# Batches on consecutive partitions, four plain stores and two loads of x

## The chip, the cores and the metric

The kernel runs on one core of a Trainium2 chip. The metric is the device time of one execution in microseconds (us), as the median of three runs. TensorE is written PE, VectorE DVE, ScalarE ACT, GpSimd POOL and SyncE SP.

## The reference

One decoding step for a batch of 8. A normalised x goes through attention over a window of 1024 cached positions (32 query heads, 8 key heads, 128 wide) and an output projection; beside it x goes through a gated feed-forward block; the two results are multiplied and added to x.

```python
B, Sq, D = 8, 1, 512;  Hq, Hkv, Sk, Dh = 32, 8, 4096, 128;  F = 1792     # all bf16
W = min(4096, max(256, Sk // 4))                                          # 1024
xn = layernorm(x)
q = (xn @ wq)                                # per head
p = softmax(q @ k[:, :, Sk - W:].T * Dh ** -0.5)
s = (p @ v[:, :, Sk - W:]) @ wo
g = silu((gelu(x @ w_gate) * (x @ w_up)) @ w_down)    # B's x is the normalised x
return x + s * g                             # (8, 1, 512)
```

## The kernel before

**Loads.** Some 47 MB are loaded, nearly all of it by SP. The order of issue is the program's: the first quarter of wo (`wo_first`, L106), wq as one load of 4 MB (L109), then for each batch two loads of 1 MB of k and two of v (`load_cache`, L84), then w_gate, w_up (L426) and w_down (L429), and the rest of wo in five loads (L439), the last three of them 640, 256 and 128 KB. ACT issues x alone, in five loads of two or one rows (L79). The destinations of the big loads are a ring of eight slots, and the loads share eight semaphores in turn, which are called lanes here: a load that takes a lane waits for the landing of the load eight places before it, whichever queue issued that.

**The head.** DVE takes the mean and variance of x with one batch on each of 8 partitions (L145 to L152). PE turns the normalised rows into columns (L166), and four copies lay them into `xnR` (L168): for each of four chunks 32 columns, of which the batches take every fourth (`RB = 4`), the rest being zero. So every result with batches on partitions has batch b on partition 32 t + 4 b, where t is the chunk of columns. `xpad` is a mask that lays x itself out in the same way for the last addition (`x_res`). The query product (L260) takes `xnR` as its stationary operand; casts, DVE transposes and 16 copies on DVE and ACT (L283) sort q into `qbd`.

**The batches.** For each batch DVE transposes k in blocks of 32 (`turn_k`, L248), PE makes the scores (L309), DVE and ACT the softmax, DVE transposes the probabilities (L344), and PE applies v (L354). Twice, after four batches each, `regroup` writes the head outputs to `oT` (L395), again with a batch on every fourth of 32 columns.

**The tail.** The gate and up products (L453), GELU, the down product (L482) and the SiLU are made while the rest of wo comes in. The output projection (`s_ps`, L501) runs over 32 blocks of wo rows, four column chunks each, in the order in which wo lands. Two DVE operations follow (`y`, L509, and `out_sb`, L511), and one store takes every fourth partition of `out_sb` (L513):

```python
    nc.sync.dma_start(
        out=out_f.rearrange("b (t d) -> t b d", t=4), in_=out_sb[0 : P : RB, :]
    )
```

L541 is the closing block, in which SP waits for all semaphores in turn and the engines meet.

Of the kernel before, what the change touches and what calls it, by code (L numbers as in the profile page):

```python
# [13 lines left out]
PSUM = bass.MemoryType.PSUM  # L14

N_SLOTS = 8
RB = 4
NEG = -1.0e30


# [1 line left out]
def kernel(  # L22
# [13 lines left out]
    nc = tc.nc  # L36

    B, Sq, D = A_x.shape
# [7 lines left out]
    P = nc.NUM_PARTITIONS  # L46
    NK = D // P
    HG = 4
    NG = Hkv // HG
# [4 lines left out]
    DT = D // 4  # L54
# [20 lines left out]


    x_sb = keep.tile([B, D], BF16, name="x_sb")
    for r, z in ((0, 2), (2, 4), (4, 6), (6, 7), (7, 8)):
        nc.scalar.dma_start(out=x_sb[r:z], in_=A_x.flatten_outer_dims()[r:z])  # L79

    def load_cache(cache, b, name):
# [15 lines left out]
    def load_v(b):  # L97
# [21 lines left out]
        out=ident,  # L119
        in_=ident,  # L120
# [4 lines left out]
        channel_multiplier=1,  # L125
# [3 lines left out]
    xnR = keep.tile([P, NK, 4, 32], BF16, name="xnR")  # L129
# [4 lines left out]
        out=xpad,  # L134
        in_=xpad,
# [1 line left out]
        fill=1.0,  # L137
        base=0,
        pattern=[[-1, 32]],
        channel_multiplier=RB,  # L140
    )


# [9 lines left out]
        out=xhat,  # L153
# [8 lines left out]
    with tc.tile_pool(name="ps_x", bufs=1, space=PSUM) as ps_x:  # L162
        xnT_ps = ps_x.tile([P, NK, B], BF16, name="xnT_ps")
        xv = xhat.rearrange("b (p k) -> b k p", k=NK)
        for k in range(NK):
            nc.tensor.transpose(xnT_ps[:, k, :], xv[:, k, :], ident[0:B, 0:B])  # L166
        for j in range(4):
            nc.vector.tensor_copy(out=xnR[:, :, j, 0 : RB * B : RB], in_=xnT_ps)  # L168
        xr_ps = ps_x.tile([P, DT], FP32, name="xr_ps")
        for t in range(4):  # L170
            nc.tensor.matmul(
                xr_ps[32 * t : 32 * t + 32, :],
                xpad,
                x_sb[:, t * DT : (t + 1) * DT],
                start=True,
                stop=True,
            )
        nc.scalar.copy(out=x_res, in_=xr_ps)  # L178
# [3 lines left out]
    qd = Hq // NG  # L182
# [6 lines left out]
        out=hv,  # L189
        in_=hv,  # L190
# [4 lines left out]
        channel_multiplier=1,  # L195
    )
    nc.gpsimd.affine_select(
        out=neg_st,
        in_=neg_st,
# [4 lines left out]
        channel_multiplier=-1,  # L204
# [3 lines left out]
        out=neg_mv,  # L208
        in_=neg_mv,
# [4 lines left out]
        channel_multiplier=1,  # L214
# [6 lines left out]
    for g in range(NG):  # L221
        nc.vector.tensor_reduce(
            out=sel[:, g, g * qd : (g + 1) * qd],
            in_=ident.rearrange("p (t g h) -> p g h t", t=4, g=NG)[:, g],
# [5 lines left out]
        out=own, in_=ident.rearrange("p (i e) -> p e i", e=8), axis=AX.X, op=ALU.add  # L230
    )
    pick = consts.tile([P, 4 * NU], BF16, name="pick")
    with nc.allow_low_precision(reason="sums of zeros and a single one"):
        nc.vector.tensor_reduce(
            out=pick, in_=ident.rearrange("p (a e) -> p a e", e=8), axis=AX.X, op=ALU.add
        )
    oT = keep.tile([P, 8, NU, 32], BF16, name="oT")
# [5 lines left out]
    qbd = keep.tile([P, 2, B, 2, NG, 4 * Hq], BF16, name="qbd")  # L243
    kT = {}

    def turn_k(b, g):
        t = kT_pool.tile([P, ROW], BF16, name="kT")
        nc.vector.transpose(out=t.bitcast(I32), in_=k_sb[b][:, g].bitcast(I32))  # L248
        kT[b, g] = t
# [5 lines left out]
    q_t = q_both[:, ROW : 2 * ROW]  # L255
    with tc.tile_pool(name="ps_q", bufs=1, space=PSUM) as ps_q:
# [10 lines left out]
        for half in range(2):  # L267
            for i in range(4 * half, 4 * half + 4):
                e = nc.vector.tensor_copy if i % 4 == 3 else nc.scalar.copy
                e(out=q_bf[:, i * 512 : (i + 1) * 512], in_=q_ps[i])  # L270
            for i in range(4 * half, 4 * half + 4, 2):
                sl = slice(i * 512, (i + 2) * 512)
                nc.vector.transpose(out=q_t[:, sl].bitcast(I32), in_=q_bf[:, sl].bitcast(I32))

    wq_ctx.close()
    q_v = q_t.rearrange("p (g h m b r w) -> p m b r w g h", g=NG, h=qd, m=2, b=B, r=RB)
    for j in range(4):
        sl = slice(32 * j, 32 * j + 32)
        for m in range(2):
            for g in range(NG):  # L280
                e = nc.scalar.copy if (4 * j + 2 * m + g) % 3 == 2 else nc.vector.tensor_copy
                c0 = j * Hq + g * qd
                e(out=qbd[sl, m, :, :, g, c0 : c0 + qd], in_=q_v[sl, m, :, 0, :, g, :])  # L283
    turn_k(0, 1)


# [89 lines left out]
    def regroup(q):  # L376

        rc = two.tile([P, 1], FP32, name="rc")
        nc.vector.reciprocal(out=rc, in_=o_ps[q][:, Dh : Dh + 1])
        o_x = two.tile([P, 8, Dh], BF16, name="o_x")  # L380
        nc.vector.scalar_tensor_tensor(
            out=o_x,
            in0=o_ps[q][:, 0:Dh].unsqueeze(1).broadcast_to([P, 8, Dh]),
            scalar=rc,
            in1=own.unsqueeze(2).broadcast_to([P, 8, Dh]),
            op0=ALU.mult,
            op1=ALU.mult,
        )
        ox_v = o_x.rearrange("p h (e j) -> p j (h e)", j=8)
        r_ps = ps_g.tile([P, 8, 4, NU], FP32, name="r_ps")  # L390
        for j in range(8):
            nc.tensor.matmul(  # L392
                r_ps[:, j], ox_v[:, j], pick, start=True, stop=True
            )
        nc.vector.tensor_copy(  # L395
            out=oT[:, :, :, 4 * RB * q : 4 * RB * (q + 1) : RB],
            in_=r_ps.rearrange("p j b u -> p j u b"),
        )

# [2 lines left out]
    for b in range(B):  # L402
        if b + 2 < B:
            load_k(b + 2)
        if b + 1 < B:
            load_v(b + 1)
            turn_k(b + 1, 0)
        softmax(b)
        if b + 1 < B:
            scores(b + 1, 0)  # L410
        if b >= 1:
            gather(b - 1)
        if b + 1 < B:
            turn_k(b + 1, 1)
            scores(b + 1, 1)
        turn_p(b)
        values(b)
        keep_o(b)
        if b == 4:
            regroup(0)  # L420
# [10 lines left out]
    for u in range(1, NU):  # L431
        if u % 2 == 1:
            pair = slot("wo_sb").rearrange("p (v j d) -> p v j d", v=2, d=D)
        t = pair[:, (u - 1) % 2]
# [6 lines left out]

    gather(B - 1)
    regroup(1)
    actx.close()

# [3 lines left out]
    for n, ws in (("z_ps", wgu[0]), ("u_ps", wgu[1])):  # L449
# [15 lines left out]
        out=z2, in0=z2, scalar1=0.044715, scalar2=1.0, op0=ALU.mult, op1=ALU.add  # L465
# [11 lines left out]
        out=hT.rearrange("p j b -> p (j b)"), in_=h_bf.rearrange("p (y j) -> p j y", j=NJ)  # L477
    )
    f_ps = ps_f.tile([P, DT], FP32, name="f_ps")
    for j in range(NJ):  # L480
# [11 lines left out]
        out=g_sb, in0=g_sb, scalar1=0.5, scalar2=0.5, op0=ALU.mult, op1=ALU.add  # L492
# [5 lines left out]
    for u in range(NU):  # L498
# [11 lines left out]
    out_sb = ffn.tile([P, DT], BF16, name="out_sb")  # L510
    nc.vector.tensor_tensor(out=out_sb, in0=y, in1=x_res, op=ALU.add)  # L511
    out_f = out.flatten_outer_dims()
    nc.sync.dma_start(  # L513
        out=out_f.rearrange("b (t d) -> t b d", t=4), in_=out_sb[0 : P : RB, :]
    )


# [28 lines left out]
```

## Time and profile before

| what | value |
|---|---|
| median of 3 runs | 120.96 us (120.95 to 120.99) |
| the profiled execution | 120.95 us, its span 119.1 us |
| busy PE, DVE, ACT, POOL | 69.2, 75.7, 32.9, 3.2 us |
| loaded, and rate over the span | 47.46 MB, 399 GB/s |
| share of the span on the chain that ended last | DMA 77%, PE 11%, DVE 6% |
| mean granted TensorE clock | 0.882 |

Busy times overlap, and the share that matters is that on the chain: the profile follows the last event back to what released it. In the slices each digit stands for a fortieth of the span, 2.98 us, in tenths; the row DMA is the mean share of the 16 DMA engines that were moving data. A line of the timeline gives start, duration, engine, line, operation, destination and source. "ACTq" and "SPq" are issues on ACT's and SP's queue; an issue is the instruction that hands over a transfer, a landing its completion.

### The profile page before, as it was taken

Reading aid. Unit: us, or ns where it says so; the run is one execution under the profiler, and the core shown is the slowest. Engines: PE = TensorE matmul, PEld = TensorE weight load, DVE = VectorE, ACT = ScalarE, POOL = GpSimd, SP = SyncE. Lnnn points to the kernel's source line nnn. Section 1 sums busy time; section 2 is a strip of 40 time slices with the busy share of each in tenths; the row PEclk is TensorE's granted clock in tenths of the full one; section 3 lists DMA queues with packets and bytes.
Section 4 is the critical chain, followed back from the end, with each engine's and each line's share of the span. In section 5 each row is a group of like instructions: output and inputs, shape, how many; then the busy total and the mean of one; then the engine's idle time right before and its main releaser. Section 6 shows DMA issues by size and latency. Waiting matters only on the chain.

```text
span 119.1 us, 1740 instructions
## 1 busy us (share of the span) xinstructions
PE 69.2 (58%) x704; PEld 33.7 (28%) x704; DVE 75.7 (64%) x101; ACT 32.9 (28%) x83; POOL 3.2 (3%) x10
## 2 busy tenths in 40 slices
PE   0000079921699497996967866657358264746550
PEld 0000033400234153442533324233124142206530
DVE  1000487999994999999987995981996114373100
ACT  1300230196100816154261441161081810110000
POOL 2000052000000000000000000000000000000000
PEclk9999999999558999999999999999999855555775
DMA  2998899999999999999999999999999999999930
GB/s 56 474 496 386 369 429 432 424 424 432 426 418 432 429 421 421 432 426 424 427 421 424 429 432 429 421 426 426 421 429 435 444 429 424 433 418 413 421 118 3
DMA packets 6108, 47.57 MB, mean 399 GB/s; under 512 B 717, under 2 KB 853, under 8 KB 1109
## 3 DMA queue, kind: packets, MB, share of 16 engines
q1 hardware_dynamic: 6084, 47.46, 94.6%
q8 instruction: 5, 0.08, 0.2%
q14 instruction: 3, 0.02, 0.0%
q10 hardware_dynamic: 16, 0.01, 0.0%
HBM read 47.46 MB, written 0.01 MB: 399 GB/s over the span
## 4 chain that ended last, share of the span: by engine, by line
DMA 77%; PE 11%; DVE 6%; ACT 2%; ACTq 1%; issue 1%; DVEq 0%; SPq 0%
DMA k_sb<-in_A_k_cache_dram 32%; DMA wo_sb<-in_A_wo_dram 19%; DMA v_sb<-in_A_v_cache_dram 16%; DMA x_sb<-in_A_x_dram 9%; PE q_ps L260 7%; DVE kT L248 4%; PE S_ps L309 2%; ACTq L79 1%; ACT L161 1%; DVE mx L319 1%; PE O_ps L354 1%; DVE stats L145 1%; PE s_ps L501 1%; PE r_ps L392 1%; DVE y L509 0%
## 5 line engine op out<-in xcount | busy, mean ns | idle before, releaser
L309 PE MATMUL S_ps<-kT,qbd 128*128 128x512 bf16 x128 | 33.0, 403 | 17.8 <-DVE kT L248 14.3
L248 DVE STREAM_TRANSPOSE kT<-k_sb 128x2048 int32<-128x2048 int32 x16 | 36.5, 2289 | 4.1 <-DMA k_sb<-in_A_k_cache_dram 4.1
L309 PEld LDWEIGHTS <-qbd 128*128 128x128 bf16 x128 | 12.8, 101 | 35.9 <-issue 19.9
L329 ACT ACTIVATE nb<-m 32x1 f32<-32x1 f32 x32 | 6.4, 201 | 23.7 <-DVE m L326 23.4
L319 DVE TENSOR_REDUCE mx<-S_ps 128x1 f32<-128x1024 f32 x8 | 9.6, 1195 | 2.5 <-PE S_ps L309 2.5
L332 ACT ACTIVATE P_sb<-S_ps,nb 128x1024 bf16<-128x1024 f32 x8 | 11.1, 1388 | 0.3
L354 PE MATMUL O_ps<-v_sb,pT 128*32 128x256 bf16 x256 | 9.3, 292 | 2.7 <-DVE pT L344 2.7
L166 PE MATMUL xnT_ps<-ident,xhat 8*128 8x8 bf16 x4 | 0.3, 174 | 15.0 <-DVE xhat L152 15.0
L260 PE MATMUL q_ps<-wq_sb,xnR 128*128 128x512 bf16 x32 | 8.7, 438 | 0.5 <-ACT x_res L178 0.5
L366 ACT COPY O_sb<-O_ps 128x256 f32<-128x256 f32 x8 | 3.0, 374 | 21.1 <-PE O_ps L354 21.1
L354 PEld LDWEIGHTS <-pT 128*32 128x32 bf16 x256 | 6.5, 102 | 6.3 <-issue 3.0
L145 DVE BATCH_NORM_STATS2 stats<-x_sb 8x6 f32<-8x512 bf16 x1 | 0.7, 681 | 11.8 <-DMA x_sb<-in_A_x_dram 11.8
L344 DVE STREAM_TRANSPOSE pT<-P_sb 128x512 int32<-128x512 int32 x8 | 5.7, 711 | 3.4 <-ACT P_sb L332 2.8
L374 PE MATMUL o_ps<-O_sb,sel 128*32 128x129 f32 x32 | 5.5, 297 | 1.0 <-ACT O_sb L366 1.0
L298 PE MATMUL S_ps<-neg_mv,neg_st 128*128 128x512 bf16 x16 | 4.8, 382 | 2.1 <-DVE q_both L270 2.1
L270 ACT CAST q_both<-q_ps 128x512 bf16<-128x512 f32 x6 | 3.0, 611 | 7.3 <-PE q_ps L260 7.3
L260 PEld LDWEIGHTS <-xnR 128*128 128x128 bf16 x32 | 3.5, 109 | 5.4 <-issue 2.2
L166 PEld LDWEIGHTS <-xhat 8*128 8x128 bf16 x4 | 0.2, 114 | 15.0 <-DVE xhat L152 15.0
L374 PEld LDWEIGHTS o_ps<-O_sb,sel 128*32 128x32 f32 x32 | 3.1, 116 | 4.3 <-issue 2.5
L501 PE MATMUL s_ps<-wo_sb,oT 128*32 128x128 bf16 x96 | 2.8, 260 | 2.4 <-DMA wo_sb<-in_A_wo_dram 2.4
L251 DVE MEMSET qbd<- 128x4096 uint32 x1 | 3.5, 3472 | 0.8 <-issue 0.8
L501 PEld LDWEIGHTS <-oT 128*32 128x32 bf16 x128 | 3.0, 124 | 3.0 <-issue 2.9
(64 smaller groups left out, 48.6 us busy)
## 6 DMA issues: line engine op xcount, KB each, us to landing
k_sb<-in_A_k_cache_dram SPq DMA_DIRECT2D x16, 1024.0 KB, 19.5
v_sb<-in_A_v_cache_dram SPq DMA_DIRECT2D x16, 1024.0 KB, 19.6
wq_sb<-in_A_wq_dram SPq DMA_DIRECT2D x1, 4096.0 KB, 14.2
wo_sb<-in_A_wo_dram SPq DMA_DIRECT2D x2, 1024.0 KB
wgu_sb<-in_B_w_gate_dram SPq DMA_DIRECT2D x1, 1792.0 KB
wgu_sb<-in_B_w_up_dram SPq DMA_DIRECT2D x1, 1792.0 KB
wd_sb<-in_B_w_down_dram SPq DMA_DIRECT2D x1, 1792.0 KB, 25.0
wo_first<-in_A_wo_dram SPq DMA_DIRECT2D x1, 1024.0 KB, 4.9
```

What stands on the lines that cost most here:

```text
L248: nc.vector.transpose(out=t.bitcast(I32), in_=k_sb[b][:, g].bitcast(I32))
L251: nc.vector.memset(qbd, 0.0)
L260: nc.tensor.matmul(q_ps[i], xnR[:, k, :, :].rearrange("p j b -> p (j b)"), wq_sb[k][:, i * 512 : (i + 1) * 512], start=(k == 0), stop=(k = ...
L298: nc.tensor.matmul(S[b][:, half, :], neg_st.rearrange("p j h -> p (j h)"), neg_mv.rearrange("p a n -> p (a n)"), start=True, stop=False,)
L309: nc.tensor.matmul(S[b][:, half, :], qbd[:, m, b, w, g, :], kv[:, half * 16 : (half + 1) * 16, m, :, w], start=False, stop=(g == NG - 1 an ...
L319: nc.vector.tensor_reduce(out=mx, in_=S[b].rearrange("p a c -> p (a c)"), axis=AX.X, op=ALU.max)
L329: nc.scalar.mul(nb[32 * j : 32 * j + 32, :], m1, -inv)
L332: nc.scalar.activation(out=P_sb[b].rearrange("p c i w -> p c w i"), in_=S[b].rearrange("p a (c w i) -> p (a c) w i", w=2, i=32), func=ACT.Exp,
L344: nc.vector.transpose(out=pT[b].rearrange("p c h w -> p (c h w)").bitcast(I32), in_=P_sb[b].rearrange("p c i w -> p (c i w)").bitcast(I32),)
L354: nc.tensor.matmul(O_ps[b][32 * t : 32 * t + 32, :, :], pT[b][:, c // 2, :, c % 2], vv[:, c, :, :], start=(c < 4), stop=(c >= C - 4),)
L374: nc.tensor.matmul(o, sel[:, g, :], O_sb[b][:, g, :], start=(g == 0), stop=(g == NG - 1))
L501: nc.tensor.matmul(s_ps[32 * t : 32 * t + 32, :], oT[:, j, u, :], wo[u][:, j, t * DT : (t + 1) * DT], start=(u == 0 and j == 0), stop=(u = ...
```

## The change

The batches take consecutive columns: `RB` goes, `xnR`, `xpad`, `oT` and the reads of q follow. So the result has batch b of chunk t on partition 32 t + b, and the store becomes four stores of 8 rows with 256 B each, chunks 0 and 1 issued by SP, 2 and 3 by ACT. x comes in two loads of four rows.

```diff
--- before.py
+++ after.py
@@ -14,7 +14,6 @@
 PSUM = bass.MemoryType.PSUM
 
 N_SLOTS = 8
-RB = 4
 NEG = -1.0e30
 
 
@@ -75,7 +74,7 @@
 
 
     x_sb = keep.tile([B, D], BF16, name="x_sb")
-    for r, z in ((0, 2), (2, 4), (4, 6), (6, 7), (7, 8)):
+    for r, z in ((0, 4), (4, 8)):
         nc.scalar.dma_start(out=x_sb[r:z], in_=A_x.flatten_outer_dims()[r:z])
 
     def load_cache(cache, b, name):
@@ -137,7 +136,7 @@
         fill=1.0,
         base=0,
         pattern=[[-1, 32]],
-        channel_multiplier=RB,
+        channel_multiplier=1,
     )
 
 
@@ -165,7 +164,7 @@
         for k in range(NK):
             nc.tensor.transpose(xnT_ps[:, k, :], xv[:, k, :], ident[0:B, 0:B])
         for j in range(4):
-            nc.vector.tensor_copy(out=xnR[:, :, j, 0 : RB * B : RB], in_=xnT_ps)
+            nc.vector.tensor_copy(out=xnR[:, :, j, 0:B], in_=xnT_ps)
         xr_ps = ps_x.tile([P, DT], FP32, name="xr_ps")
         for t in range(4):
             nc.tensor.matmul(
@@ -273,14 +272,14 @@
                 nc.vector.transpose(out=q_t[:, sl].bitcast(I32), in_=q_bf[:, sl].bitcast(I32))
 
     wq_ctx.close()
-    q_v = q_t.rearrange("p (g h m b r w) -> p m b r w g h", g=NG, h=qd, m=2, b=B, r=RB)
+    q_v = q_t.rearrange("p (g h m r b w) -> p m r b w g h", g=NG, h=qd, m=2, b=B, w=2)
     for j in range(4):
         sl = slice(32 * j, 32 * j + 32)
         for m in range(2):
             for g in range(NG):
                 e = nc.scalar.copy if (4 * j + 2 * m + g) % 3 == 2 else nc.vector.tensor_copy
                 c0 = j * Hq + g * qd
-                e(out=qbd[sl, m, :, :, g, c0 : c0 + qd], in_=q_v[sl, m, :, 0, :, g, :])
+                e(out=qbd[sl, m, :, :, g, c0 : c0 + qd], in_=q_v[sl, m, 0, :, :, g, :])
     turn_k(0, 1)
 
 
@@ -393,7 +392,7 @@
                 r_ps[:, j], ox_v[:, j], pick, start=True, stop=True
             )
         nc.vector.tensor_copy(
-            out=oT[:, :, :, 4 * RB * q : 4 * RB * (q + 1) : RB],
+            out=oT[:, :, :, 4 * q : 4 * (q + 1)],
             in_=r_ps.rearrange("p j b u -> p j u b"),
         )
 
@@ -510,9 +509,10 @@
     out_sb = ffn.tile([P, DT], BF16, name="out_sb")
     nc.vector.tensor_tensor(out=out_sb, in0=y, in1=x_res, op=ALU.add)
     out_f = out.flatten_outer_dims()
-    nc.sync.dma_start(
-        out=out_f.rearrange("b (t d) -> t b d", t=4), in_=out_sb[0 : P : RB, :]
-    )
+    for t, e in ((0, nc.sync), (2, nc.scalar), (1, nc.sync), (3, nc.scalar)):
+        e.dma_start(
+            out=out_f[:, t * DT : (t + 1) * DT], in_=out_sb[32 * t : 32 * t + B, :]
+        )
 
 
 # ---- launch: one core; inputs and outputs as the reference has them ----
```

## The prediction

> **What bounds the kernel now.** I read the page's slices first, then the chain of waits, the timeline of the tail, the waits of the SP queue and the answer on the tile `x_sb`; packets, landings and issues of single transfers come from the trace's own records.
>
> ```profile
> DMA  2998899999999999999999999999999999999930
> GB/s 56 474 496 386 369 429 432 424 424 432 426 418 432 429 421 421 432 426 424 427 421 424 429 432 429 421 426 426 421 429 435 444 429 424 433 418 413 421 118 3
> ```
>
> The load stream runs from the second slice to the 38th with no hole. The first row of `wo_first` starts at 1.83 us and the last load has landed at 115.43, and 47.46 MB pass in between at a flat 420 to 430 GB/s. So the end of the loads is a sum of bytes, which this change leaves alone.
>
> ```profile
> 2.24 10.74 DMA x_sb<-in_A_x_dram
> ...
> 16.03 8.69 PE q_ps L260 x32
> ...
> 43.21 20.13 DMA k_sb<-in_A_k_cache_dram
> 63.34 0.02 issue
> 63.36 2.31 DVE kT L248
> ...
> 92.78 22.30 DMA wo_sb<-in_A_wo_dram
> 115.09 0.04 issue
> 115.13 0.66 PE s_ps L501 x11
> 115.79 0.02 issue
> 115.81 0.30 DVE y L509
> 116.12 0.02 issue
> 116.14 0.29 DVE out_sb L511
> ```
>
> The chain begins with x, but it leaves the engines at 24.7 us and then runs through landings. At 63.36 the transpose of k waits for a load that landed that moment, so whatever the engines had lost or won before is forgotten there. At the end the last piece of wo lands, and s_ps, y and out_sb follow.
>
> ```profile
> 116.46 0.70 SPq L513 DMA_DIRECT2D out_dram<-out_sb  x1
> ```
>
> ```profile
> SPq L84 <- DMA x_sb<-in_A_x_dram: 5.0, 3, 1.9
> SPq L541 <- DMA out_dram<-out_sb: 0.8, 1, 0.8
> ```
>
> The store is the last link, and only this link is plainly in series. Its issue takes 0.699 us (116.459 to 117.158). Its first packet starts 0.602 us later (117.760), the last of 32 rows of 256 B starts at 117.916 and the last 4-byte packet at 117.930. There are four of those, so four streams carry eight rows each. The semaphore is complete at 118.265, 0.335 us behind that last packet. SP sees it at 118.281, and the closing waits end the span at 119.1. The profiled execution takes 120.95 us, 1.85 us more than its span; the median of three runs is 120.96, so I add 0.01 to a sum made against the profile.
>
> **The x loads.** Three of five issues on ACT's queue go.
>
> ```profile
> L79 ACTq DMA_DIRECT2D x_sb<-in_A_x_dram x5: 237/275/532, 0.8 to 2.2; - x5
> ```
>
> The first took 0.532 us, the second 0.237. The landings were at 2.11, 5.74, 8.08, 10.51 and 12.99 us: an x row or its 4-byte semaphore packet gets its turn on a stream after one packet of wq, 1.21 us for 32 KB, and the first stream carried all five loads one after another. Two loads have the place of the first two, so x is complete at about 5.7 us instead of 12.99, if four rows spread over four streams as two did over two. From x landed to the last xnR copy took 12.99 to 15.85, 2.86 us, so xnR would be ready near 8.6. q_ps then waits for wq, which landed at 15.43, and starts at about 15.5 instead of 16.03. DVE's fills, which stood behind xnR up to 22.14, come before wq. The engines win about 0.55 us here.
>
> On the end I cost this at nothing, because the k load that lands at 63.34 releases the engines there and the stream ends by its bytes. Were that cover gone, it would be 0.55 us faster. SP's loads that today wait for a lane held by x (issued at 8.09, 10.53, 13.00) go out earlier, into a stream that is full with wq until 15.0, so they gain nothing. Packet work shifts too: the first stream loses three rows and three semaphore packets (3 × 52 + 3 × 9 ns, 0.18 us), two others gain about 0.12 us each. The 16 streams' last landings lie between 113.71 and 115.43 us, so which one is last is decided by larger things; bounds −0.18 and +0.12, taken as 0.
>
> **The layout.** The xnR copies (0.22 us each), the xpad mask, 16 qbd copies (0.36 on DVE, 0.615 on ACT) and two oT casts (0.43) keep counts and sizes and only change strides. Were all eleven DVE copies of qbd a tenth dearer or cheaper, that is 0.4 us at 28 to 31 us, covered by the same load at 63.34; the second oT cast ends at 101.8 and its first user starts at 109.7. Nothing. The matmuls have the same tiles.
>
> **The store.** One issue of 0.699 us with a two-dimensional destination goes. On each of two queues come two issues with a plain list of eight rows, one behind the other; what queues behind them is only the closing block at L541. ACT has been idle since 110.3 and out_sb releases it with SP. The trace has no plain small store, so I bound it.
>
> - First issue on a queue: 0.24 (second x load) to 0.70 (today's store). For ACT, the nearest row is its own first x load, 0.53; for SP, its late plain loads, 0.33.
> - Second issue: 0.24 to 0.38 (the x loads behind the first). I take 0.26 on ACT and 0.33 on SP.
> - End of issue to first packet: 0.395 (first x load, 1.333 to 1.728) to 0.602 (the store). I take 0.395, since the x load is the plain one.
> - Packets: eight rows over eight streams give one row per stream and store, 0.03 instead of 0.17.
> - Last packet to landing: 0.31 (x) to 0.335 (store). I take 0.335, the write.
>
> ACT: 116.46 + 0.53 + 0.04 + 0.26 + 0.395 + 0.03 + 0.335 = 118.05. SP: 116.46 + 0.33 + 0.05 + 0.33 + 0.395 + 0.03 + 0.335 = 117.93. ACT decides, 0.215 before today's 118.265. SP's closing waits pass through seven steps of about 65 ns, and only the last of them waited. They are done today at 117.5, before any landing, so I add nothing for four semaphores in place of one. All lower ends give 117.72 (−0.54), all upper ends 118.55 (+0.29). Sum: 120.95 − 0.21 = 120.74, as a median 120.75 us.
>
> The Trainium skill, "DMA: Bandwidth & Descriptors", section Specifications, gives a first-byte latency of about 0.6 us on the sync and scalar path. The store's row agrees with it and the x row lies below; as an estimate by that page in place of 0.395 the sum would come to 120.95, no gain.
>
> **The rivals.**
> *No gain from the delay.* If the 0.602 us belongs to writes and not to the two-dimensional pattern, ACT ends at 118.26 and the time stays 120.95. For it: the same kind of transfer; against it: today's streams prepare eight rows each. 0.17.
>
> *Short issues.* If 0.53 us was the price of the very start and a plain issue costs 0.24 everywhere, the landing is at 117.72 and the time 120.42. For it: four of five x issues took 0.24 to 0.38. 0.20.
>
> *The two queues get in each other's way (slower).* At the start, when both queues issue at once, SP's first k load took 0.646 us against 0.535 later, and ACT's last x load 0.379 against 0.237. If first issues cost 0.70 and second ones 0.38, and the delay is 0.602, the landing is at 118.55 and the time 121.25. It decides as soon as the last issue ends after 117.50 with the short delay, or 117.30 with the long one. If the four issues ran strictly one after another (0.53 + 0.26 + 0.33 + 0.33 and gaps, to 118.05), it would be 118.81, or 121.50. Against it: SP's first 407 ns issue and ACT's 237 ns one overlapped. 0.21. The Trainium skill's same page, section Rules for kernel authors, has a rule that speaks against this change: many small transfers are to be coalesced, since below 64 KB one pays mostly overhead; by it this rival is the outcome, and the trace shows no case of four small stores at once.
>
> *The head counts.* If the 0.55 us reached the end, 120.2. Against it stand the full slices. 0.03. That x doesn't land early, because four rows share one stream, changes x alone and not the time.
>
> *The stream's end moves* by up to 0.2 us either way as packets fall differently on the slowest stream: 120.55 or 120.95. 0.05.
>
> **How the numbers follow.** The forecast keeps 0.34, from 120.60 to 120.90; the likeliest time is 120.75. What a measurement of this kernel can tell from no change is about 0.2%, 0.24 us, so 120.72 and 121.20 divide the signs. Nearly half of the forecast (0.15), the short issues (0.20), the head and a part of the stream's case (0.05) lie below 120.72: faster 0.41. The slower rival lies above 121.20 with some of its cases just inside: slower 0.21. The rest, 0.38, is no change. The range leaves out one in ten on each side: from the short issues' 120.40 to just over the slower rival's first price, 121.30.
>
> **What would show it.** In the changed profile: x landed near 5.7 us, q_ps starting when wq lands, near 15.5; the last wo piece still landing at 115.4 within 0.2; out_sb ending at 116.4; four issues of 0.24 to 0.53 us, the last ended by 117.3; the last landing near 118.05. A wo landing that moves by more than 0.3 us, an issue over 0.6 us, or a first packet 0.6 us behind its issue would each prove a step wrong.

## The result, and the profile after

The changed kernel takes 121.11 us (median of 20 runs, 120.86 to 121.46) against 120.95 us (20 runs, 120.84 to 121.20): ratio 1.0014, 95% interval 1.0008 to 1.0019. So it is slower by 0.10 to 0.23 us, where 0.2 us of gain was forecast. Its profiled execution takes 121.19 us and has a span of 119.19 us.

Slices of the changed kernel, then its chain:

```profile
DMA  3998899999999999999999999999999999999920
GB/s 70 461 495 385 374 432 429 423 429 432 426 418 429 429 423 426 429 426 423 423 423 426 432 426 429 426 421 434 415 432 429 435 447 419 423 428 415 414 103 3
```

```profile
1.29 14.10 DMA wq_sb<-in_A_wq_dram
15.39 0.14 issue
15.53 9.28 PE q_ps L259 x32
...
42.92 20.55 DMA k_sb<-in_A_k_cache_dram
63.47 0.02 issue
63.49 2.31 DVE kT L247
...
92.80 22.43 DMA wo_sb<-in_A_wo_dram
115.23 0.04 issue
115.27 0.29 PE s_ps L500 x8
115.56 0.01 issue
115.58 0.32 PE s_ps L500 x4
...
116.25 0.29 DVE out_sb L510
```

The stream is as full as before. x has left the chain; it now begins with wq. The engines again wait for a k load at 63.47, and wo ends the chain 0.11 us later than in the first profile (last landing 115.534 against 115.426).

The tile `x_sb`, the timeline of the tail and SP's waits:

```profile
L78 ACTq DMA_DIRECT2D x_sb<-in_A_x_dram x2: 260/418/575, 0.8 to 1.4; - x2
```

```profile
116.57 0.71 SPq L513 DMA_DIRECT2D out_dram<-out_sb  x2
116.57 0.65 ACTq L513 DMA_DIRECT2D out_dram<-out_sb  x2
```

```profile
SPq L541 <- DMA out_dram<-out_sb: 0.8, 4, 0.4
```

A merged timeline line runs from the first issue's start to the last one's end. In the records SP's issues take 0.362 and 0.299 us and ACT's 0.297 and 0.310, against 0.699 for the one before. SP now waits four times in the closing block. The four landings are complete at 117.764 (chunk 2, ACT), 117.966 (chunk 0, SP), 118.165 (chunk 3, ACT) and 118.362 (chunk 1, SP): 1.796 us from the first issue to the last landing, against 1.806 with one store. The store has gained nothing.

### The profile page after: what moved, and what is told of

Same layout as the page of the kernel before. It is cut to its first block, busy times and chain, and to the rows that moved or that the text cites. A ratio compares the mean times of both kernels' runs of the same rounds, so it can differ in the third digit from the quotient of the medians.

```text
span 119.2 us, 1739 instructions
## 1 busy us (share of the span) xinstructions
PE 69.6 (58%) x704; PEld 33.4 (28%) x704; DVE 75.7 (63%) x101; ACT 32.9 (28%) x83; POOL 3.2 (3%) x10
## 4 chain that ended last, share of the span: by engine, by line
DMA 79%; PE 11%; DVE 6%; issue 0%; SPq 0%
DMA k_sb<-in_A_k_cache_dram 32%; DMA wo_sb<-in_A_wo_dram 19%; DMA v_sb<-in_A_v_cache_dram 16%; DMA wq_sb<-in_A_wq_dram 12%; PE q_ps L259 8%; DVE kT L247 4%; PE S_ps L308 2%; DVE mx L318 1%; PE O_ps L353 1%; PE s_ps L500 1%; PE r_ps L391 1%; SPq L105 0%; DVE y L508 0%; DVE out_sb L510 0%; DVE oT L394 0%
## 5 line engine op out<-in xcount | busy, mean ns | idle before, releaser
L259 PE MATMUL q_ps<-wq_sb,xnR 128*128 128x512 bf16 x32 | 9.3, 461 | 7.4 <-DMA wq_sb<-in_A_wq_dram 7.4
L269 DVE CAST q_both<-q_ps 128x512 bf16<-128x512 f32 x2 | 1.3, 672 | 3.9 <-ACT q_both L269 3.9
```

What stands on the lines that cost most here:

```text
L259: nc.tensor.matmul(q_ps[i], xnR[:, k, :, :].rearrange("p j b -> p (j b)"), wq_sb[k][:, i * 512 : (i + 1) * 512], start=(k == 0), stop=(k = ...
```

## The experiments

All times are medians; "landed" counts from the start of the first store's issue. The table has every profile that the text draws on: SP's instructions in the trace, the profiled execution, its span, their difference, the last landing of wo, and the time from the first issue of a store to the last landing. These are single executions; where the rows matter, the text below adds the averages over all executions of a kernel. The runs whose names begin with tail_ and that leave a part of the result unstored have one execution each.

```
kernel                 SP   us      span     outside  wo landed  store landed
before                 72   120.95  119.094  1.856    115.426    1.806
before_again           72   120.95  119.003  1.947    115.328    1.813
x_two_only             72   121.23  119.375  1.855    115.524    1.806
stores_four_only       73   122.56  120.534  2.026    115.520    2.842
after_x_five           73   121.59  119.468  2.122    115.473    1.817
after                  73   121.19  119.186  2.004    115.534    1.796
after_again            73   121.15  119.168  1.982    115.505    1.807
tail_one_of_four       72   120.55  118.689  1.861    115.433    1.208
tail_two_of_four       72   120.76  118.905  1.855    115.526    1.401
tail_second_to_sbuf    72   121.10  119.249  1.851    115.477    1.204 (SP's)
tail_rows_apart        72   120.62  118.762  1.858    115.423    1.355
tail_three             73   121.12  119.093  2.027    115.509    1.618
tail_four_on_sp        75   121.60  119.545  2.055    115.429    2.258
one_store_dve          72   121.39  119.535  1.855    115.486    1.318
one_store_dve_pool     72   121.09  119.234  1.856    115.283    1.315
two_stores_dve         72   121.51  119.648  1.862    115.567    1.837
one_store_shared       73   121.19  119.165  2.025    115.416    1.311
two_stores_shared      72   120.96  119.104  1.856    115.510    1.419
before_sp_drain        73   121.01  119.003  2.007    115.340    1.807
after_wo_first_act     72   121.05  119.193  1.857    115.524    1.805
```

**The parts by themselves.** Theory A: the x loads make the stream end later. Theory B: the stores cost more than one. Theory C: the layout costs.

x_two_only, on the kernel before:

```diff
-    for r, z in ((0, 2), (2, 4), (4, 6), (6, 7), (7, 8)):
+    for r, z in ((0, 4), (4, 8)):
```

> The kernel before with x in two loads of four rows and nothing else changed. The changed kernel's profile puts its loss of 0.1 us in the last landing of wo (115.53 us against 115.43), and none in the store (issue to landing 1.80 against 1.81). Theory A, the loads: the two x loads shift lanes and streams, and the stream ends 0.1 us later: time +0.10 to +0.15 us (ratio 1.001), last wo landing near 115.53. Theory B, the stores: time as before, last wo landing 115.43. Theory C, the layout: as B here. All three: x landed at 5.6 us, q_ps starts at 15.5, xnR ready near 8.6.

121.18 us, ratio 1.0013 (1.0005 to 1.0022). The wo landing of the profile agrees with A, but the larger part is behind the store. Its landing takes 1.806 us as ever, and SP sees it at 118.377; then SP steps through four more entries of its closing list before its drain at 118.690, 0.313 us instead of 0.129 (118.281 to 118.410). Three loads fewer ahead of the store have moved its semaphore three places forward in that list. Over the 11 executions of this kernel the span is on average 0.21 us longer than over the 21 of the kernel before beside it (119.33 and 119.12 us). If those 0.18 us of the closing list recur in each, 0.02 us is left for the loads, and theory A with its 0.1 us isn't borne out.

stores_four_only, on the kernel before:

```diff
-    nc.sync.dma_start(
-        out=out_f.rearrange("b (t d) -> t b d", t=4), in_=out_sb[0 : P : RB, :]
-    )
+    for t, e in ((0, nc.sync), (2, nc.scalar), (1, nc.sync), (3, nc.scalar)):
+        e.dma_start(
+            out=out_f[:, t * DT : (t + 1) * DT], in_=out_sb[32 * t : 32 * t + 32 : RB, :]
+        )
```

> The kernel before with its store cut in four plain stores of eight rows (every fourth partition of each block of 32), two on SP and two on ACT; x stays in five loads, batches stay on every fourth partition. Theory A: time as before within 0.1 us; last out_sb end 116.43, issues of 0.30 to 0.36 us, landings of the four stores about 0.2 us apart, last landing 1.80 us after the first issue begins. Theory B: +0.15 us, with the last landing later than 1.81 us behind the first issue. Theory C: as A.

122.35 us, ratio 1.0114 (1.0100 to 1.0127). None of the three had it: A and C expected 0.30 to 0.36 us an issue, B 0.15 us in all. The tile `out_sb` in this kernel, minimum, median and maximum of an issue in ns:

```profile
L514 SPq DMA_DIRECT2D out_dram<-out_sb x2: 687/738/790, 116.6 to 117.4; - x2
L514 ACTq DMA_DIRECT2D out_dram<-out_sb x2: 652/693/734, 116.6 to 117.3; - x2
```

and in the changed kernel:

```profile
L513 SPq DMA_DIRECT2D out_dram<-out_sb x2: 299/330/362, 116.6 to 117.0; - x2
L513 ACTq DMA_DIRECT2D out_dram<-out_sb x2: 297/304/310, 116.6 to 116.9; - x2
```

Both have eight rows of 256 B a store and a one-dimensional list on the result's side. The step of the partitions differs, four against one; x comes in five loads here, but after_x_five, with the same five loads and consecutive partitions, has issues of 0.299 to 0.368 us. So strided partitions are enough for an issue of 0.7 us, and the two-dimensional destination, to which the prediction put it, isn't needed for it; what that destination costs from consecutive partitions no run shows. Nor does a store of a quarter issue faster than the whole one with the same step (0.652 to 0.790 us against 0.699).

The issues are only a part of the loss. The first packet comes 0.647 and 0.648 us behind ACT's issues, and 0.865 and 0.903 behind SP's, against 0.45 to 0.53 in the changed kernel. Why it is later on SP, whose issue ends 0.05 to 0.10 us behind ACT's, is not shown. From the last 4-byte packet to the landing the four stores take 0.334 to 0.339 us, as a single one does; they land 0.275 us apart and more. The last landing comes at 2.842 us, and it has the first entry of SP's closing list, which adds 0.31.

after_x_five is the changed kernel with x back in five loads.

> The changed kernel with x back in five loads: new layout and four stores. Theory A: 120.95 us as before, last wo landing 115.43. Theory B: 121.1 us, last wo landing 115.43 and the loss behind out_sb. Theory C: 121.1 us, with the loss ahead of out_sb, in last landings or s_ps.

121.43 us, ratio 1.0036 (1.0023 to 1.0050), more than any theory gave. Its stores land in 1.817 us, like the changed kernel's, but with three loads more ahead of it the last store has the first entry of SP's closing list. SP sees it at 118.339, steps on through six entries, and drains at 118.783: 0.444 us, against 0.122 in the changed kernel (118.379 to 118.501).

```profile
SPq L541 <- DMA out_dram<-out_sb: 1.1, 1, 1.1
```

One wait of 1.1 us at the head of the list stands where the changed kernel has four in a row near its end. The parts don't add: from 120.97 the four stores alone cost 1.38 us, the layout under them gives back 0.92 (121.43), and the two x loads then give back 0.36 (121.07, the next run), though by themselves they cost 0.21.

after_again is the changed kernel unchanged.

> The changed kernel once more, for its noise and a second profile. All theories: 121.1 us, ratio 1.001. Theory A: the last wo landing is at 115.5 again; if it is at 115.43 here, the 0.1 us of the first profile was chance and the median's loss has to be somewhere else.

121.07 us, ratio 1.0011 (1.0002 to 1.0020), and the same tail to 0.02 us.

**What one plain store costs, and the order of landings.** before_again is the kernel before. The next three keep part of the stores and store only that part of the result:

```diff
-    for t, e in ((0, nc.sync), (2, nc.scalar), (1, nc.sync), (3, nc.scalar)):
+    for t, e in ((0, nc.sync), (2, nc.scalar)):       # tail_two_of_four; tail_one_of_four: chunk 0 alone
...
+            out=out_f[:, t * DT : (t + 1) * DT] if t == 0 else spare[0:B, :], ...  # tail_second_to_sbuf
```

> The kernel before once more, for a second profile of it. If the last wo landing is near 115.5 us here, as in the five profiles of other kernels (115.47 to 115.53), the first profile of before (115.43) was an early one, and the 0.1 us ahead of out_sb is not the change's. If it is at 115.43 again, something in all the changed programs ends the stream later. Ratio 1.000 either way; the store from issue to landing 1.81 us.

120.93 us, ratio 0.9996 (0.9987 to 1.0005), the stream's end at 115.328.

> The changed kernel with only the store of chunk 0, by SP; three quarters of the result are not stored. One plain store alone: issue 0.30 to 0.36 us, first packet 0.45 to 0.49 behind it, landing 0.33 behind its last 4-byte packet, so landed 1.2 us after its issue begins (1.80 with four). Theory O, the landings of one set of streams are ordered and each costs 0.2 us: 1.2 us. Theory Q, each queue is slow by itself: also 0.2 us later here, 1.4 us.

Landed after 1.208 us, as theory O expected, and not after the 1.4 of theory Q: issue 0.368, first packet 0.426 later, the last 4-byte packet 0.072 behind that, landing 0.342 behind it.

```profile
116.47 0.37 SPq L513 DMA_DIRECT2D out_dram<-out_sb  x1
```

> The changed kernel with only chunk 0 by SP and chunk 2 by ACT; half of the result is not stored. Theory O: the one that comes second lands 0.17 to 0.20 us behind the first although its packets are only 0.02 us later, and the end is at 1.4 us from the issue. If both land within 0.05 us of each other, the spacing in the full tail came from the second issues and not from the order of the landings.

ACT's landing is complete at 117.757, SP's at 117.955, 0.198 us later, though SP's packets run only 0.02 us behind (117.348 and 117.366). SP's landing comes 0.517 us behind its last packet instead of 0.342.

> As the run with two stores, but ACT's transfer of chunk 2 goes to a spare tile in the core's own memory instead of the result; three quarters of the result are not stored. Theory O (order of landings on the same streams): SP's store still lands later than 0.33 us behind its last packet, by 0.1 to 0.2. Theory R (two writes into the same rows of the result get in each other's way): SP's store lands 0.33 us behind its last packet, 1.2 us from its issue.

This told nothing apart. The transfer within the core took 0.727 us to issue, its packets started at 117.836, and SP's store had landed by 117.657. tail_rows_apart asked the question again:

```diff
+            out=out_f[2 * t : 2 * t + 4, t * DT : (t + 1) * DT], in_=out_sb[34 * t : 34 * t + 4, :]   # t = 0 SP, 2 ACT
```

> Two stores at once as in the run with chunks 0 and 2, but each of four rows and in different rows of the result: SP stores batches 0 to 3 of chunk 0, ACT batches 4 to 7 of chunk 2; a quarter of the result is stored. Both go on the same four streams. Theory O (landings on the same streams are ordered): SP's store lands 0.15 to 0.20 us behind ACT's, although its packets come 0.02 later, 0.45 to 0.50 behind its last packet. Theory R (writes into the same rows of the result hinder each other): both land 0.33 us behind their last packets, within 0.05 us of each other.

ACT's landing 117.629, SP's 117.812: 0.183 us apart, with packets 0.018 apart and no row in common. Theory R falls; the spacing goes with two stores in flight at once. That they use the same streams is not shown: each has four 4-byte packets, but the records don't name a packet's stream. The Trainium skill, "DMA: Bandwidth & Descriptors", section Queues, rings and completion order, says that the semaphore increment of a transfer lands only after every earlier write of that DMA engine, across its queues. The trace agrees with such an order; the price, 0.18 to 0.20 us for a store whose packets come just behind another's, is the trace's own. In stores_four_only, where the landings are further apart, nothing is added.

tail_three leaves out chunk 3; tail_four_on_sp puts all four on SP.

> The changed kernel with three of its four stores: chunks 0 and 1 by SP, 2 by ACT; a quarter of the result is not stored. In all four profiles with four stores the execution is 1.98 to 2.12 us longer than its span, in nine of the ten others 1.85 to 1.86 (1.95 in the tenth). Theory N, the number of stores or the second issue on a queue costs outside the span: 1.95 to 2.1 here. Theory A2, it takes the second issue on ACT: 1.86. Landings: chunk 1 lands 0.33 to 0.37 us behind its last packet, near 1.6 us from the first issue, as nothing of ACT lands just ahead of it.

> The changed kernel with all four stores on SP. Issues 0.36 and three of 0.30 with 0.05 between them; the fourth ends 1.4 us after the first begins, and lands 0.9 to 1.0 behind: 2.35 to 2.45 us from the first issue against 1.80, so +0.6 us in the span, ratio 1.005 to 1.006. Outside the span, theory N: 2.0; theory A2: 1.86, and the ratio 0.001 lower.

Three stores land in 1.618 us, as expected. Without ACT's second store just ahead, chunk 1 lands 0.36 us behind its last packet, against 0.486 in the changed kernel. Four on SP land in 2.258 us, 0.1 to 0.2 under what was expected, at 121.64 us, ratio 1.0050 (1.0036 to 1.0064). So ACT's queue is worth 0.46 us of the tail. Both have about 2.03 to 2.06 us outside the span, which speaks for theory N here, before the next run.

**Versions that might win.** They have the new layout, and x in five loads unless said otherwise, and put chunks side by side on partitions 0 to 7, so that fewer plain stores suffice; y and x_res are as before.

```diff
-    nc.vector.tensor_tensor(out=out_sb, in0=y, in1=x_res, op=ALU.add)
...
+    out_sb = ffn.tile([B, D], BF16, name="out_sb")       # one_store_dve
+    for t in range(4):
+        r = slice(32 * t, 32 * t + B)
+        nc.vector.tensor_tensor(
+            out=out_sb[:, t * DT : (t + 1) * DT], in0=y[r, :], in1=x_res[r, :], op=ALU.add
+        )
+    nc.sync.dma_start(out=out_f, in_=out_sb)
```

> A version that may beat both: new layout, x in five loads, and the last addition made by four DVE operations of 8 partitions x 128 that write chunk t beside chunk 0, on partitions 0 to 7, so that one plain store of eight rows of 1 KB suffices. DVE: four operations of about 0.17 us apart and 0.29 for the last, 0.8 instead of 0.29. Store: 1.2 us from issue to landing, as the single plain store had, instead of 1.81, and its lane is the last in the closing list. Sum: +0.5 - 0.6 = -0.1 us, 120.85. If an operation on 8 partitions costs the full 0.33 us a step, +1.0 - 0.6, 121.35.

> As the version with one store, with three of the additions on DVE and one on POOL beside them. If POOL takes its one in under 0.6 us: DVE 0.63 instead of 0.29, store 1.2 instead of 1.81: -0.27 us, 120.7. If POOL is slower or the two engines hold each other up, it ends later by what POOL exceeds 0.63.

> Four DVE additions of 8 partitions that put chunks 1 and 3 beside 0 and 2 in two tiles, and two plain stores of eight rows of 512 B: ACT's after two additions, SP's after all four. x in five loads. ACT lands early, SP's issue starts as in the version with one store, its landing 1.2 us later, +0.0 to 0.05 if ACT's landing is over by then. Same as the version with one store or up to 0.1 us slower through the closing list (one lane more); never faster, if only the last store counts.

121.33 (1.0016 to 1.0040), 121.23 (1.0017 to 1.0042) and 121.49 us (1.0032 to 1.0058). The timeline of the first shows why:

```profile
116.20 1.16 DVE L513 TENSOR_TENSOR out_sb<-y,x_res 8x128 bf16<-8x128 f32 x4
117.39 0.37 SPq L516 DMA_DIRECT2D out_dram<-out_sb  x1
```

Four additions on 8 partitions take 1.16 us, 0.28 each, about the 0.29 of one on 128. The store then lands in 1.32 us, so 0.87 us is spent to save 0.49.

The shared versions make one addition on all partitions and move the rest with three engines at once (one_store_shared: DVE, POOL and an ACT copy) or two (two_stores_shared: DVE and POOL, x in four loads).

> A version that may beat both: new layout, x in five loads; the addition on all partitions stays and gives chunk 0 in its place, and chunks 1, 2 and 3 are put beside it on partitions 0 to 7 by three engines at once: DVE and POOL by an addition of 8 x 128 (0.29 and 0.45 us), ACT by a copy (0.24). out_sb ready 0.33 to 0.45 us later than one addition, one plain store of eight rows of 1 KB lands in 1.2 to 1.3 us instead of 1.81 and has the last lane. Sum -0.1 to -0.25 us, 120.75 to 120.85, ratio 0.998 to 0.999. If the engines hold each other up, as DVE did beside POOL (0.35 a step instead of 0.29), nothing is won.

> As the version before it, with chunk 1 put beside 0 by DVE and chunk 3 beside 2 by POOL and two plain stores of eight rows of 512 B, chunks 2 and 3 by ACT, 0 and 1 by SP; x in four loads, so that the stores have the last two lanes. Ready 0.33 us later than today, first landing in 1.2 us, the second up to 0.2 behind: -0.05 to -0.25 us. Expected 0.05 us behind the single store, for the order of the landings.

121.21 us, ratio 1.0017 (1.0008 to 1.0026), and 120.96 us, ratio 0.9996 (0.9987 to 1.0004). DVE's addition beside POOL's takes 0.42 us instead of 0.29, as in one_store_shared:

```profile
116.28 0.45 POOL L512 TENSOR_TENSOR out_sb<-y,x_res 8x128 bf16<-8x128 f32 x1 [97.88 <-DVE y L508]
116.45 0.42 DVE L515 TENSOR_TENSOR out_sb<-y,x_res 8x128 bf16<-8x128 f32 x1
```

The two-store version equals the kernel before; none beats it.

**Outside the span.** one_store_shared has one store and 2.025 us outside its span, so the number of stores, theory N, isn't it. What goes with the difference in all eighteen profiles to that point is SP's instruction count: 1.85 to 1.86 us with 72 (1.95 once, where the last semaphore update in the trace, too, comes 0.09 us later behind the span), 1.98 to 2.12 with 73 or 75. Two runs to test it:

```diff
+    nc.sync.drain()                                      # before_sp_drain: behind load_v(0), on the kernel before
-    nc.sync.dma_start(out=wo_first, in_=wo_src[0])       # after_wo_first_act, on the changed kernel
+    nc.scalar.dma_start(out=wo_first, in_=wo_src[0])
```

> The kernel before with one more instruction on SP's queue, a drain behind the first v load, where SP waits anyway. In the eleven profiles with 72 instructions of SP the execution exceeds the span by 1.85 to 1.86 us (1.95 in one, which shows 0.09 us more behind its span); in the seven with 73 or 75 by 1.98 to 2.12, whatever the number of stores (one store with 73: 2.03). Theory P, the length of SP's program costs outside the span: 73 here, 2.0 us outside, time +0.12 to +0.17 us, ratio 1.0010 to 1.0014, with the store and the stream as before. If the ratio is 1.000 and the difference 1.86, the stores or the new layout carry it.

> The changed kernel with the first load of wo issued by ACT behind x, so that SP has 72 instructions again; all four stores stay. Theory P: 1.86 us outside the span, time 0.12 to 0.17 us under the changed kernel's, 120.95, ratio 1.000 (0.9992 to 1.0004). If the stores carry it: 2.0 us outside, ratio 1.0014. The first load of wq begins at 0.81 instead of 1.29 and lands earlier by what wo_first then takes later; the stream's end stays, 115.4 to 115.5.

The part outside the span does what was expected in both: 2.007 us with the drain, 1.857 us with four stores and 72 instructions. The times follow only half. before_sp_drain: 121.01 us, ratio 1.0009 (1.0000 to 1.0018), a little under the 1.0010 to 1.0014 expected. after_wo_first_act: 121.11 us, ratio 1.0019 (1.0008 to 1.0030), not the 120.95 expected.

Every execution has its span on record, to 0.1 us, so the two parts can be told apart in all of them:

```
kernel                  SP   executions   outside: mean, range    span: mean
before, in five sets    72   94           1.87   1.81 to 2.00     119.10 (sets 119.07 to 119.13)
two_stores_shared       72   11           1.88   1.82 to 1.93     119.09
x_two_only              72   11           1.85   1.81 to 1.89     119.33
after_wo_first_act      72   11           1.88   1.82 to 1.92     119.31
after                   73   20           2.01   1.95 to 2.13     119.13
after_again             73   11           2.02   1.95 to 2.14     119.08
one_store_shared        73   11           2.00   1.97 to 2.04     119.22
before_sp_drain         73   11           2.02   1.98 to 2.09     119.04
tail_four_on_sp         75   4            2.10   2.08 to 2.14     119.55
```

The part outside follows the count both ways: one drain more adds 0.13 us to it (1.88 beside it in its set), and one issue moved from SP to ACT takes 0.14 away, with all four stores in place. So after_wo_first_act kept its loss inside the span, 119.31 us on average against 119.07 in its set. Issuing wo_first on the other queue also moves wq's start, so this run changes more than the count; where in the span it loses is not shown, as its profiled execution, 119.19, is one of the shorter ones. The changed kernel's span is that of the kernel before to within 0.05 us: its loss is the time outside. (For the kernel before's 20 executions of the first measurement no spans are on record; the five sets ran beside the experiments.) Why an instruction more on SP costs there is not shown.

## Why the prediction was wrong, step by step

Two steps failed, and together they make nearly all of the 0.36 us between 120.75 and 121.11: the sum for the last landing (0.21 us) and the time outside the span, which was carried over unchanged (0.14). The signs that the prediction named for the head, the stream and the issues came; the last landing, 118.36 us instead of 118.05, didn't.

**The bound: right.** Loads fill the stream in every profile, and x's early landing didn't reach the end. x was complete at 5.60 us (5.7 forecast), xnR ready at 8.3 (8.6), q_ps started at 15.53 (15.5). Even before_sp_drain, whose q_ps ended at 26.15 us, has its last wo landing at 115.34.

**The head's rows: the saving came, its cost lay elsewhere.** Taken as 0 on the end, the x loads moved the store's place in the closing list. (A row of x took 0.044 to 0.046 us in the trace before, not the 0.052 of the packet sum, which was taken as 0 in any case.) The step that said "I add nothing for four semaphores in place of one" is right for this change, by luck of the count: 0.122 us from the last landing's being seen to SP's drain, against 0.129. It was right for none of the parts alone (0.184 and 0.315 us more).

**The store: wrong, and this is the 0.2 us of the forecast.** The failed step is "ACT decides, 0.215 before today's 118.265": SP's landing decides, and it comes 1.796 us behind its first issue, not 1.59. Both sums ran from the issue's start. ACT's came out at 1.59 us and measured 1.594, but only because its errors cancel: the issues cost 0.297 and 0.310 instead of 0.53 and 0.26, the first packet came 0.488 us behind the issue instead of 0.395, and the landing 0.391 behind the last packet instead of 0.335. SP's came out at 1.47 us and measured 1.796, and it decides. Its issues were priced well (0.362 and 0.299 for two of 0.33). The terms mis-sized are: issue to first packet 0.534 instead of 0.395 (0.14), packets 0.070 instead of 0.03 (0.04), last packet to landing 0.486 instead of 0.335 (0.15).

The 0.395 came from the nearest row, a load of x; a second store on SP without ACT's beside it has 0.483 (tail_three), so about 0.05 of the 0.534 goes with the other queue. Most of the excess behind the last packet is the order of landings, which no term of the sum had: without ACT's store just ahead it is 0.360 instead of 0.486. The rival without gain foretold the tail that came, but by a delay of 0.602 us; for plain stores it is 0.43 to 0.53. The short issues came in part, 0.30 to 0.36 us, but not at 0.24.

**The slower rival: the sign, not the mechanism.** No issue was delayed by the other queue; 0.36 and 0.30 us were nearly the same with SP alone (0.357 to 0.293). What the other queue delays is the landing, and the first packet a little. By the Trainium skill's rule on coalescing, which stood beside it ("DMA: Bandwidth & Descriptors", section Rules for kernel authors), many small transfers are to be made one. The runs agree where the shape stays: from strided partitions one store takes 1.81 us and four 2.84; plain, one of 8 KB takes 1.31 to 1.32 and four of 2 KB on two queues 1.80. The change came out even because it went from one strided store to four plain ones.

**What the sum had no place for: the loss.** "The profiled execution takes 120.95 us, 1.85 us more than its span" was carried over to the changed kernel, and nothing said why it should stay. Over 20 executions it is 2.01 us in the changed kernel, against 1.87 in the kernel before; this goes with SP's 73rd instruction, as the last two runs show both ways, and is about all of the measured 0.10 to 0.23 us.

The two profiles alone would mislead here. From the first of before to that of the changed kernel the execution grew by 0.24 us: 0.15 outside the span and 0.11 ahead of out_sb, less 0.01 in the store. The second pair gives 0.20 us: 0.03 outside, as before_again's happened to be long, and 0.18 ahead of out_sb. But the last wo landing lies between 115.28 and 115.57 us over all twenty profiles, on average 115.49 with x in two loads (10 profiles) and 115.43 in five (9), and over all executions the spans agree: 119.13 and 119.08 us for the changed kernel, 119.07 to 119.13 for the kernel before. So the part ahead of out_sb was mostly chance of single executions.

## What to carry to other kernels

Price a small store by its shape on the core's side first: the same eight rows took 0.30 to 0.37 us to issue from consecutive partitions and 0.65 to 0.79 from every fourth. Cutting one transfer into several on two queues did not shorten an issue, and the last landing pays for the second issue and for landings that queue behind each other, so count to the last landing of the later queue. And when a kernel is compared within 0.3%, look at what any added or removed transfer does to the closing list and to the time outside the span, before giving the difference to the edit that was meant; and take both from many executions, as one profile of each kernel can put the loss in another place.

## What the runs showed of the hardware

- Two stores in flight at once land 0.18 to 0.20 us apart, with packets 0.02 us apart, from different queues and in different rows.
- SP's closing list costs about 0.06 us for each entry behind the last landing, up to 0.44 us with its drain.
- With 73 instructions on SP an execution was on average 2.00 to 2.02 us longer than its span (six kernels), with 75 2.10, with 72 1.85 to 1.92 (kernels with several executions). tail_four_on_sp, with 75, has an 8 KB instruction packet at 121.4 us, behind its span; the other profiles show none, so that this is a fetch of SP's program is not shown.
- q_ps took 8.6 to 10.0 us for the same 32 matmuls: in the records of the granted clock, full speed begins at 18.7 to 22.1 us, and PE ran at half pace until then (a matmul every 0.43 us instead of 0.22). It cost the end nothing here.
- A DVE addition of 8 x 128 takes 0.28 us where one of 128 x 128 takes 0.29, and 0.42 beside one on POOL (0.45 us).
